# Weight chunks of the first layer decoded in pairs that make their sums on the spot, and a planner with other transfer times, in a one-core attention and two-layer kernel

## The chip, the cores and the metric

The kernel runs on 1 core of one Trainium2 chip. The metric is the device time of one execution in microseconds (us); less is better. TensorE is written PE, its weight loads PEld, VectorE DVE, ScalarE ACT, SyncE SP. SP issues every DMA of this kernel, in one order.

## The reference

What is computed: attention over keys and values that are first averaged over 8 neighbours, then two layers of matrix products.

```python
# q, k, v: [8 batches, 8 heads, 576, 64]
k_p = k.reshape(B, H, 72, 8, D).mean(axis=3)
v_p = v.reshape(B, H, 72, 8, D).mean(axis=3)
attn = softmax(scale * q @ k_p.T)          # sum + 1e-9 below
x = (attn @ v_p), heads side by side       # [4608, 512]
h = x @ w_in;  g = maximum(0.01 * h, h);  x = g @ w_out          # w_in 512x2048, w_out 2048x512
h = x @ w2_in; g = h * clip(h + 3, 0, 6) / 6;  out = g @ w2_out  # the same sizes
```

## The kernel before

**The work and its order.** The 4608 tokens are 9 tiles of 512. Attention is cut into 32 units (batch, pair of head groups, half of the queries), whose scores (matmul L465), transposes (L540, L558) and value products (L585) are strewn between the matmuls of the layers. PE multiplies each f32 operand as a high and a low part, three matmuls in place of one.

Tiles 0, 1 and 2 go through the first layer directly: for each of 16 chunks f of 128 hidden units, 12 matmuls into the hidden values (`gemm1`, L702 to L704), a leaky step on ACT (L717), a split on ACT (L299) and DVE (L309), and 12 matmuls into y (`gemm2`, L751 to L753). This is done in four passes: **pass 1** takes tile 0 through the first `mid` = 9 chunks and stores the unfinished y; **pass 2** takes tile 1 through all 16; **pass 3** takes tile 0 through the chunks from `mid` on and adds; **pass 4** takes tile 2 through all 16. In the profile pass 1 runs from 32 to 107 us, pass 2 to 209, pass 3 to 267, pass 4 to 384. Everything later (`Pair1` for the other six tiles of layer one, then `Pair` for layer two) multiplies blocks of 2x2 with seven products in place of eight (L974). For these seven products the weights have to be summed and differenced beforehand; the results (`left1`, `left2`) are kept in DRAM and streamed back (L1011).

**The weights.** `weights(f)` loads the 1024 KB of chunk f (L608), decodes the 64-bit numbers to f32 in `decode` (two ACT instructions L617, L619 and two DVE instructions L622, L630, each 128x1024), and splits the result into the tile `w{f}` (ACT L299, DVE L309, 128x1024). `keep` then stores the decoded chunk, 512 KB, to DRAM (L651) and three pieces of 256 KB of the split to `left1` (L663). Raw words and the decoded chunk lie in tiles that belong to later chunks, in turn.

`first_weights(f)`, for f = 0 to 7, reads chunks f and f+8 back from DRAM in four pieces of 256 KB (L929) into a tile `raw`, and `combine` makes the sums from its four quarters: four DVE sums or differences (L873), each followed by `split_off`, which splits it (ACT L299, DVE L309) into a tile `st` and stores that in two DMAs of 256 KB (L900). `second_weights(f)` does the same for layer two from the input (L944, 2 x 1024 KB): a decode in four halves of 128x512, each with a temporary tile `st`, three split_offs and `combine`. There are **2** tiles `raw`, which keys and values of attention use too, and **3** tiles `st`: a fourth `st` can be written when the stores from the first have landed. `C` lists in which slot of which pass each of these jobs stands: `when0`, `when1` for `weights`, `left1` for `first_weights`, `left0`, `left2` for `second_weights`, `att*` for units of attention.

**The order on the engines.** Every piece of work is put into a `Plan` with an engine, a cost in ns and its reads and writes. `Plan.order` places them all by these costs and the delays of `lag` between two engines, PE in program order, the other engines and SP by how soon each piece is due, and the instructions are written out in that order; each engine then runs its own in order. A DMA costs `nbytes / 350 + 50`, what reads its result may start 900 ns later, and a DMA may follow an engine's result after 1250 ns. In the start-up the plan also puts small idle matmuls where it expects PE to wait (L1521).

Of the kernel before, what the change touches and what calls it, by code (L numbers as in the profile page):

```python
# [28 lines left out]
ROUNDS = 12  # L29
C = dict(  # L30
    n32=4,
    flex=652,
    mid=9,
    half0=3,
    steps0='rfrfffrff',
    when0=[0, 0, 3, 3, 7, 14, 16, 16],
    att0=[0, 0, 11, 36],
    sec0=4,
    half1=4,
    steps1='frrffrfffffffrff',  # L40
    when1=[0, 8, 10, 20, 22, 25, 35],
    att1=[0, 0, 7, 32],
    sec1=6,
    att2=[0, 4],
    quick=[0, 2, 2, 2, 6],
    slow=[0, 5, 5, 5, 5],
    left0=[(0, 13), (1, 20)],
    left1=[[(0, 26), (1, 30)], [(2, 0), (3, 2), (4, 10)], [(5, 4), (6, 6), (7, 16)]],
    att3=[0, 3, 6, 9, 12, 15, 18, 21],
    gaps3=[0, 3, 3, 3, 3],  # L50
    prep3=[22, 25],
    att5=[6, 15, 24, 33, 42, 51, 60, 69],
    gaps5=[0, 8, 8, 8, 8],
    prep5=[78, 88],
    att7=[8, 24, 40, 56],
    gaps7=[0, 10, 10, 10, 10],
    prep7=[76, 88],
    left2=[[(2, 24)], [(3, 30), (4, 43)], [(5, 0), (6, 16), (7, 32)]],
)
WARM_FROM = 2700  # L60
ENGINES = ("pe", "act", "dve", "gp", "dma")
# [32 lines left out]
class View:  # L94


    def __init__(self, buf, key, cut):
        self.buf, self.cut = buf, cut
        self.key = () if key is None else key if isinstance(key, tuple) else (key,)

    def ap(self):
        t = self.buf.get()
# [3 lines left out]
class Plan:  # L106
# [17 lines left out]
    def add(self, engine, cost, emit, reads=(), writes=(), other=None):  # L124

        n = len(self.tasks)
        after = set()
        over = lambda d, key: (t for k, v in d.items() if all(a == b for a, b in zip(k, key)) for t in v)
        for v in (*reads, *writes):
            assert not v.buf.gone, v.buf.name  # L130
            if v.buf.prev is not None:
                after |= v.buf.prev.users
        for v in reads:
            before = set(over(v.buf.writers, v.key))
            assert before, v.buf.name
            after |= before
        for v in writes:
            after.update(over(v.buf.writers, v.key))
            after.update(over(v.buf.readers, v.key))
        after.discard(n)  # L140
        for v in reads:
            v.buf.readers.setdefault(v.key, set()).add(n)
            v.buf.users.add(n)
        for v in writes:
            v.buf.writers.setdefault(v.key, set()).add(n)
            v.buf.users.add(n)
        self.tasks.append(([(engine, cost, emit)] + ([other] if other else []), after))

    def lag(self, a, b):

        return self.LAG.get((a, b), 900 if a == "dma" else 1250 if b == "dma" else 180)

    def place(self, ways, after, then, rank, lag, first):

# [89 lines left out]
def attention_moe_moe(ctx: ExitStack, tc: tile.TileContext, qt, kt, vm, vr, wt, wq, eye, mask, out):  # L244
# [27 lines left out]
    def act_cost(n, psum=False):  # L272
        return n / 1.2 + (51 if psum else 93)
# [14 lines left out]
        add("pe", n, emit, reads, writes)  # L288

    def on_dma(nbytes, emit, reads, writes):  # L290
        add("dma", nbytes / 350 + 50, emit, reads, writes)

    def other(*way):
        return way if len(plan.tasks) < C["flex"] else None

    def copy(dst, src, n, psum=False, scale=None):

        if scale is None:
            a = lambda: ACT.copy(out=dst.ap(), in_=src.ap())  # L299
            b = lambda: DVE.tensor_copy(out=dst.ap(), in_=src.ap())  # L300
        else:
            a = lambda: ACT.mul(out=dst.ap(), in_=src.ap(), mul=scale)  # L302
            b = lambda: DVE.tensor_scalar_mul(dst.ap(), src.ap(), scale)
        add("act", act_cost(n, psum), a, [src], [dst], other("dve", dve_cost(n, not psum), b))

    def subtract(dst, a, b, n):
        on_dve(
# [96 lines left out]
    def prep_k(u):  # L404
        held_keys[u.g] = u.b
        if u.early:
            for i in range(2):
                sum_pool(part(u.ks, i, lambda t, i=i: t[:, 72 * i : 72 * i + 72]), half_k(u, i), 72)
        else:
            sum_pool(u.ks, u.k, 144)  # L410
        for e in range(2):
            p = slice(64 * e, 64 * e + 64)
            c = slice(SP * e, SP * e + SP)
            s = View(u.ks.buf, u.ks.key, lambda t, p=p: pair(u.ks.cut(t))[p])
            copy(part(kbd[u.g], e, lambda t, p=p, c=c: t[p, :, c]), s, 144)

    def prep_v(u):
        vh, vl = vbd[u.g]
# [6 lines left out]
        for e in range(2):  # L425
            p = slice(64 * e, 64 * e + 64)
            s = View(u.vs.buf, u.vs.key, lambda t, p=p: pair(u.vs.cut(t))[p])
            if u.whole32:
                copy(part(u.whole32[0], e, lambda t, p=p: t[p, :, p]), s, 128, u.early)
                continue  # L430
            hi, lo = [t(e, lambda t, p=p: t[p, :, p]) for t in (vh, vl)]
            copy(hi, s, 128)
            subtract(lo, s, hi, 128)
        on_dve(
            256,
            lambda: DVE.tensor_tensor(
                out=u.m.ap().rearrange("p (a d) -> p a d", a=4),
                in0=u.rs.ap().rearrange("p (o d) -> p o d", o=1).to_broadcast([96, 4, D]),
# [162 lines left out]

    w = {}
    left1 = []
    chunk = [buf(f"chunk{f}", [128, 1024], pool=dram) for f in range(NF)]

    def load_w(f, raw):
        on_dma(
            1 << 20, lambda: DMA.dma_start(out=raw.get().bitcast(I32), in_=wt[f].bitcast(I32)), [], [raw()]  # L608
        )

    def decode(raw, t, l, half=None):

        c0, n = (0, 1024) if half is None else (512 * half, 512)
        words = lambda: raw.get().bitcast(I32).rearrange("p (n two) -> p n two", two=2)[:, c0 : c0 + n]
        bits = lambda v: v.ap().bitcast(I32)

        on_act(n, lambda: ACT.mul(out=t.ap(), in_=f32(words()[:, :, 1]), mul=2.0**-112), [raw()], [t])  # L617

        on_act(n, lambda: ACT.mul(out=bits(l), in_=words()[:, :, 0].bitcast(U32), mul=7.49 / 2**32), [raw()], [l])  # L619
        on_dve(  # L620
            n,
            lambda: DVE.scalar_tensor_tensor(  # L622
                out=bits(l), in0=bits(t), scalar=3, in1=bits(l), op0=ALU.logical_shift_left, op1=ALU.bitwise_or
            ),
            [t, l],
            [l],
        )
        on_dve(
            n,
            lambda: DVE.scalar_tensor_tensor(  # L630
                out=bits(t), in0=bits(t), scalar=-0x80000000, in1=bits(l), op0=ALU.bitwise_and, op1=ALU.bitwise_or
            ),
            [t, l],
            [t],
        )

    def decode_w(f, raw, t, l):
# [5 lines left out]
        lo = wf("lo", lambda t: t[:, 2:4].rearrange("p a n -> p (a n)"))  # L643
        copy(hi, t, 1024)
        subtract(lo, t, hi, 1024)
        keep(f, t, wf)

    def keep(f, t, wf):

        d = chunk[f]()  # L650
        on_dma(1 << 19, lambda: DMA.dma_start(out=d.ap(), in_=t.ap()), [t], [d])  # L651
        r, lower = f % 8, f >= 8

        for g, sides in enumerate(([(5, 1)], [(1, 0), (5, 1)]) if lower else ([(0, 0), (1, 1)], [(0, 0)])):
# [264 lines left out]
    def first_weights(f):  # L919

        t = new_raw()
        for i in range(2):
            for g in range(2):
# [3 lines left out]
                def emit(i=i, g=g):  # L927
                    at = t.get().rearrange("p (i j g n) -> p i j g n", i=2, j=2, g=2)
                    DMA.dma_start(  # L929
                        out=at[:, i, :, 0, :] if g == 0 else at[:, :, i, 1, :],  # L930
                        in_=chunk[f + 8 * i].get()[:, 512 * g : 512 * g + 512].rearrange("p (j n) -> p j n", j=2),
                    )

                on_dma(262144, emit, [chunk[f + 8 * i]()], [View(v.buf, (*v.key, g), None) for v in dst])
        combine(left1[0], f, quarters(t))

    def second_weights(f):
# [398 lines left out]
    load(mask_sb, mask, 1536)  # L1336
    fetch(u1)
    add("dve", 70, lambda: DVE.memset(three.ap(), 3.0), [], [three])
    room = {0: 8, 1: 9, 2: 10, 3: 14, 4: 15, 5: 14, 6: 15, 7: 14, 8: 15, 9: 14, 10: 15, 11: 14, 12: 15, 13: 15, 14: 15}
    temps = {}  # L1340

    def weights(f):
        raw = area(room[f]) if f in room else new_raw()
        at = 12 if f % 2 == 0 and f < 12 or f == 11 else 11 if f < 11 else 14 if f < 14 else 0
        if at == 12:
            t, l = a12("w", lambda t: t[:, 1024:2048]), a13("w", lambda t: t[:, 1024:2048])
        else:
            if not at or at not in temps:
                temps[at] = area(at) if at else new_raw()
            t, l = [temps[at](i, lambda t, i=i: t[:, 1024 * i : 1024 * i + 1024]) for i in range(2)]  # L1350
        load_w(f, raw)
        decode_w(f, raw, t, l)
# [227 lines left out]
```

## Time and profile before

| | |
|---|---|
| median of 3 runs | 1623.59 us (1619.22 to 1626.57) |
| the profiled execution, its own time | 1624.79 us |
| its span, first to last instruction | 1623.0 us |
| PE busy | 1588.9 us (98%), 7899 matmuls |
| DVE busy | 1188.2 us (73%) |
| ACT busy | 1009.3 us (62%) |
| DMA | 414.73 MB, mean 256 GB/s |

The sum of PE's idle time is the span less its busy time, 34.1 us. A matmul's end is modelled, so a busy PE can still be one at half clock: the granted clock has to be read beside the busy time. Where PE waits, the engine it names is mostly not the cause, but itself stands behind something in its own order.

### The profile page before, as it was taken

How to read it: one execution, taken by the hardware profiler on the slowest of the kernel's cores; microseconds unless marked ns; L12 is line 12 of the kernel's file. 1: busy time of each engine (PE TensorE's matmuls, PEld its weight loads, DVE VectorE, ACT ScalarE, POOL GpSimd, SP SyncE). 2: the span in 40 equal slices, each digit the busy share in tenths (PEclk: the TensorE clock that was granted, in tenths of full speed). 3: DMA queues.
4: the chain of work that ended last, by engine and by line, in shares of the span. 5: the costliest groups of instructions: out<-in, count | busy, mean ns of one | idle time of the engine just before them, and what ended most of it. 6: DMA issues, size and time to landing. Idle time of an engine off the chain costs nothing.

```text
span 1623.0 us, 23182 instructions
## 1 busy us (share of the span) xinstructions
PE 1588.9 (98%) x7899; PEld 1361.6 (84%) x7899; DVE 1188.2 (73%) x2122; ACT 1009.3 (62%) x2481; POOL 2.8 (0%) x14
## 2 busy tenths in 40 slices
PE   9999999999999999999999999999999999999999
PEld 8878887887778778878877898888899889889988
DVE  7988777666788976696688669657846965784594
ACT  7977665667777677665675555556545555654454
POOL 0000000000000000000000000000000000000000
PEclk9999999999999999999999999999999999999999
DMA  8989999646886799669999656766775776567564
GB/s 304 323 289 309 325 306 300 231 154 213 259 297 228 243 313 328 220 219 304 335 340 319 215 208 239 263 214 215 262 239 207 238 262 214 214 246 234 208 233 150
DMA packets 134981, 414.73 MB, mean 256 GB/s; under 512 B 19024, under 2 KB 51920, under 8 KB 113104
## 3 DMA queue, kind: packets, MB, share of 16 engines
q1 hardware_dynamic: 134864, 413.26, 74.5%
q8 instruction: 63, 1.03, 0.3%
q14 instruction: 54, 0.44, 0.1%
HBM read 321.98 MB, written 91.23 MB: 255 GB/s over the span
## 4 chain that ended last, share of the span: by engine, by line
PE 66%; DVE 11%; DMA 9%; ACT 4%; issue 2%; SPq 1%; ACTq 0%; DVEq 0%
PE y L974 29%; PE h L974 18%; PE a L974 12%; DMA left<-st 3%; DVE w L873 2%; DMA raw<-chunk 1%; DMA raw<-vm 1%; PE a L465 1%; DVE gl L309 1%; PE a L585 1%; DMA x<-x 1%; DVE st L309 1%; PE y L751 1%; PE y L752 1%; PE y L753 1%
## 5 line engine op out<-in xcount | busy, mean ns | idle before, releaser
L873 DVE TENSOR_TENSOR w<-y,w 128x512 f32<-128x512 f32 (+2 forms) x108 | 70.3, 657 | 73.7 <-PE y L974 73.6
L302 ACT ACTIVATE gh<-w 128x460 fp32r<-128x460 f32 (+1 forms) x140 | 81.8, 587 | 66.5 <-PE y L974 35.2
L1169 DVE SCALAR_TENSOR_TENSOR gl<-w,gh 128x460 fp32r<-128x460 f32 (+1 forms) x140 | 88.5, 635 | 28.6 <-ACT gh L302 28.4
L974 PE MATMUL y<-w,xh 128*128 128x512 f32 (+2 forms) x444 | 106.0, 386 | 2.6 <-DMA xh<-left 2.2
L873 DVE TENSOR_TENSOR w<-w 128x460 f32<-128x460 f32 (+2 forms) x168 | 106.0, 648 | 2.1 <-ACT w L717 1.2
L974 PEld LDWEIGHTS y<-w,xh 128*128 128x128 f32 x444 | 83.7, 190 | 16.6 <-DMA xh<-left 2.5
L490 ACT ACTIVATE s<-a,mx 96x72 f32<-96x72 f32 x264 | 79.7, 323 | 14.1 <-DVE mx L484 14.0
L974 PE MATMUL y<-w,raw 128*128 128x460 f32 (+1 forms) x384 | 86.6, 370 | 0.0
L751 PE MATMUL y<-gh,w 128*128 128x512 f32 (+2 forms) x220 | 85.0, 386 | 0.0
L702 PE MATMUL h<-xh,w 128*128 128x512 f32 (+2 forms) x220 | 83.6, 380 | 0.0
L752 PE MATMUL y<-gl,w 128*128 128x512 f32 (+2 forms) x220 | 81.3, 369 | 2.0 <-DVE gl L309 1.9
L1140 ACT ACTIVATE gh<-w,three 128x460 f32<-128x460 f32 (+1 forms) x60 | 40.9, 682 | 67.2 <-DVE w L873 67.2
L704 PE MATMUL h<-xh,w 128*128 128x512 f32 (+2 forms) x220 | 81.8, 372 | 0.0
L703 PE MATMUL h<-xl,w 128*128 128x512 f32 (+2 forms) x220 | 81.6, 371 | 0.0
L753 PE MATMUL y<-gh,w 128*128 128x512 f32 (+2 forms) x220 | 81.0, 368 | 0.0
L299 ACT CAST gh<-w 128x512 fp32r<-128x512 f32 x96 | 59.7, 623 | 33.3 <-PE y L974 18.2
L974 PE MATMUL y<-w,xl 128*128 128x512 f32 (+2 forms) x324 | 79.0, 386 | 0.0
L974 PEld LDWEIGHTS y<-w,raw 128*128 128x128 f32 x384 | 71.9, 188 | 8.1 <-DVE w L873 0.5
L299 ACT CAST st<-raw 128x512 fp32r<-128x512 f32 x88 | 54.6, 623 | 38.4 <-DMA left<-st 22.8
L309 DVE TENSOR_TENSOR st<-raw,st 128x512 fp32r<-128x512 f32 x88 | 60.0, 686 | 21.3 <-ACT st L299 20.8
L309 DVE TENSOR_TENSOR gl<-w,gh 128x512 fp32r<-128x512 f32 x96 | 65.6, 685 | 10.5 <-ACT gh L299 10.1
L873 DVE TENSOR_TENSOR w<-h,w 128x512 f32<-128x512 f32 (+2 forms) x44 | 29.0, 663 | 59.1 <-PE h L974 59.0
(270 smaller groups left out, 4372.7 us busy)
## 6 DMA issues: line engine op xcount, KB each, us to landing
raw<-left SPq DMA_DIRECT2D x68, 1024.0 KB, 4.9
left<-st SPq DMA_DIRECT2D x176, 256.0 KB, 4.6
xh<-left SPq DMA_DIRECT2D x37, 1024.0 KB, 4.9
xl<-left SPq DMA_DIRECT2D x68, 512.0 KB, 4.9
xh<-left SPq DMA_DIRECT2D x56, 512.0 KB, 5.3
w<-left SPq DMA_DIRECT2D x56, 512.0 KB, 5.3
xl<-left SPq DMA_DIRECT2D x25, 1024.0 KB, 5.0
raw<-wq SPq DMA_DIRECT2D x16, 1024.0 KB, 7.1
```

Of the source, the lines that this page charges most:

```text
L299: a = lambda: ACT.copy(out=dst.ap(), in_=src.ap())
L302: a = lambda: ACT.mul(out=dst.ap(), in_=src.ap(), mul=scale)
L309: lambda: DVE.tensor_tensor(out=dst.ap(), in0=a.ap(), in1=f32(b.ap()), op=ALU.subtract),
L702: PE.matmul(out=o, lhsT=hi, rhs=xh.get()[:, k, c0:c1], start=k == 0, stop=False)
L703: PE.matmul(out=o, lhsT=hi, rhs=xl.get()[:, k, c0:c1], start=False, stop=False)
L704: PE.matmul(out=o, lhsT=lo, rhs=xh.get()[:, k, c0:c1], start=False, stop=k == 3)
L751: PE.matmul(out=y[:, n0:n1], lhsT=hi, rhs=gh.get()[:, n0:n1], start=start, stop=False)
L752: PE.matmul(out=y[:, c0:c1], lhsT=hi, rhs=gl.get()[:, c0:c1], start=False, stop=False)
L753: PE.matmul(out=y[:, c0:c1], lhsT=lo, rhs=gh.get()[:, c0:c1], start=False, stop=stop)
L873: on_dve(n, lambda: DVE.tensor_tensor(out=dst.ap(), in0=a.ap(), in1=b.ap(), op=op), [a, b], [dst])
L974: PE.matmul(out=o, lhsT=l, rhs=r, start=first and i == m == 0, stop=last and i == len(left) - 1 and m == 2, skip_group_check=True,)
L1169: lambda: DVE.scalar_tensor_tensor(out=lo.ap(), in0=v.ap(), scalar=1.0 / 6.0, in1=f32(hi.ap()), op0=ALU.mult, op1=ALU.subtract),
```

## The change

Chunks are taken in the order 0, 8, 1, 9, 2, 10, ... (`ORDER`), so that the two chunks whose sums are made together follow each other. `mid` is 8. The first 8 chunks in this order (hidden blocks 0 to 3 and 8 to 11) go as before, by `weights`, the store to DRAM and `first_weights`, which is now called for f = 0 to 3 only. The other 8 go in four pairs by the new `pair_weights`, all in pass 2: load both, decode each in two halves into the quarters of one tile `raw`, split each half into `w{c}`, store the three pieces to `left1`, and call `combine` at once. They are neither stored to DRAM as decoded chunks nor read back. Their raw words lie in the chunk's own tile `w{c}`, and the temporaries of the decode are tiles `st`. A `View` can now carry several keys (`also`), since half a chunk touches two quarters.

The jobs move: both `second_weights` of pass 2 go, one to pass 3 and one to pass 4; pass 2 has no `first_weights` (2 before), passes 3 and 4 have two each (3 before). The plan reckons a DMA at `nbytes / 340 + 60` and 1500 ns until its result is read; decodes on ACT cost `0.075 * n` more in the plan, and some small copies and one DVE product about 110 ns more. Slots are set anew in all passes up to the third `Pair1`.

```diff
     n32=4,
-    flex=652,
-    mid=9,
+    flex=612,
+    mid=8,
     half0=3,
-    steps0='rfrfffrff',
-    when0=[0, 0, 3, 3, 7, 14, 16, 16],
+    steps0='rfrfffrf',
+    when0=[0, 1, 0, 3, 11, 14, 16],
     att0=[0, 0, 11, 36],
     sec0=4,
     half1=4,
     steps1='frrffrfffffffrff',
-    when1=[0, 8, 10, 20, 22, 25, 35],
-    att1=[0, 0, 7, 32],
+    when1=[7, 7, 17, 20],
+    att1=[0, 0, 26, 32],
     sec1=6,
     att2=[0, 4],
-    quick=[0, 2, 2, 2, 6],
+    quick=[0, 2, 2, 2, 2],
     slow=[0, 5, 5, 5, 5],
-    left0=[(0, 13), (1, 20)],
-    left1=[[(0, 26), (1, 30)], [(2, 0), (3, 2), (4, 10)], [(5, 4), (6, 6), (7, 16)]],
...
-    left2=[[(2, 24)], [(3, 30), (4, 43)], [(5, 0), (6, 16), (7, 32)]],
+    prep7=[76, 87],
+    left2=[[(0, 10)], [(1, 16)], [(2, 28)], [(3, 26), (4, 43)], [(5, 0), (6, 16), (7, 36)]],
...
+        self.keys = [self.key, *also]
...
-        return self.LAG.get((a, b), 900 if a == "dma" else 1250 if b == "dma" else 180)
+        return self.LAG.get((a, b), 1500 if a == "dma" else 1250 if b == "dma" else 180)
...
-        add("dma", nbytes / 350 + 50, emit, reads, writes)
+        add("dma", nbytes / 340 + 60, emit, reads, writes)
...
+    ORDER = [f + 8 * i for f in range(8) for i in range(2)]
+    chunk = [buf(f"chunk{f}", [128, 1024], pool=dram) for f in range(C["mid"])]
...
-        c0, n = (0, 1024) if half is None else (512 * half, 512)
-        words = lambda: raw.get().bitcast(I32).rearrange("p (n two) -> p n two", two=2)[:, c0 : c0 + n]
-        bits = lambda v: v.ap().bitcast(I32)
-
-        on_act(n, lambda: ACT.mul(out=t.ap(), in_=f32(words()[:, :, 1]), mul=2.0**-112), [raw()], [t])
-
-        on_act(n, lambda: ACT.mul(out=bits(l), in_=words()[:, :, 0].bitcast(U32), mul=7.49 / 2**32), [raw()], [l])
+        n, a = (1024, slice(0, 4)) if half is None else (512, slice(2 * half, 2 * half + 2))
+        words = lambda: raw.get().bitcast(I32).rearrange("p (a n two) -> p a n two", a=4, two=2)[:, a]
+        cut = lambda v: v.ap() if len(v.ap().shape) == 3 else v.ap().rearrange("p (a n) -> p a n", n=256)
+        bits = lambda v: cut(v).bitcast(I32)
+        act = lambda emit, v: on_act(n, emit, [raw()], [v], False, 0.075 * n)
+
+        act(lambda: ACT.mul(out=cut(t), in_=f32(words()[:, :, :, 1]), mul=2.0**-112), t)
+
+        act(lambda: ACT.mul(out=bits(l), in_=words()[:, :, :, 0].bitcast(U32), mul=7.49 / 2**32), l)
...
-        keep(f, t, wf)
-
-    def keep(f, t, wf):
-
         d = chunk[f]()
         on_dma(1 << 19, lambda: DMA.dma_start(out=d.ap(), in_=t.ap()), [t], [d])
+        keep(f, wf)
+
+    def keep(f, wf):
+
+        f = ORDER[f]
...
+    def pair_weights(f):
+
+        t = new_raw()
+        blocks = lambda v: v.rearrange("p (q g n) -> p q g n", q=4, g=2)
+        for i in range(2):
+            c = 2 * f + i
+            words = buf(f"w{c}", [128, 2048])
+            load_w(c, words)
+
+            part = [
+                View(
+                    t,
+                    ((i, 0, g) if g == 0 else (0, i, g)),
+                    lambda v, at=at, g=g: blocks(v)[:, at, g, :],
+                    [(i, 1, g) if g == 0 else (1, i, g)],
+                )
+                for g, at in enumerate((slice(2 * i, 2 * i + 2), slice(i, i + 3, 2)))
+            ]
+            for g in range(2):
+                decode(words, part[g], new_st()(None, lambda t: t[:, 0, :]), g)
+            wf = buf(f"w{c}", [128, 4, 512], F32R)
+            w[c] = wf
+            for g in range(2):
+                hi, lo = [
+                    wf((what, g), lambda t, r=2 * r + g: t[:, r].rearrange("p (a n) -> p a n", a=2))
+                    for r, what in enumerate(("hi", "lo"))
+                ]
+                copy(hi, part[g], 512)
+                subtract(lo, part[g], hi, 512)
+            keep(c, wf)
         combine(left1[0], f, quarters(t))
...
-    for f, slot in enumerate(C["when1"], mid):
-        jobs.at(slot, lambda f=f: weights(f))
+    more_weights(jobs, pair_weights, enumerate(C["when1"], mid // 2))
     held["x"] = new_x32()
...
-    more_weights(jobs, first_weights, C["left1"][0])
-    more_weights(jobs, second_weights, C["left0"])
...
-    more_weights(jobs, first_weights, C["left1"][1])
+    more_weights(jobs, first_weights, C["left1"][0])
+    more_weights(jobs, second_weights, C["left2"][0])
...
-    more_weights(jobs, first_weights, C["left1"][2])
+    more_weights(jobs, first_weights, C["left1"][1])
+    more_weights(jobs, second_weights, C["left2"][1])
```

## Rows read from the trace of the kernel before

**Rows 1.** Windows by pass: length, busy us (instructions) per engine, PEclk, DMA share, GB/s

```profile
0.00:32.00 32.00, 29.26 (x306) 27.07 (x307) 23.42 (x55) 22.92 (x89) 2.55 (x13) 1.00 0.87 310
32.00:107.00 75.00, 71.23 (x457) 62.35 (x456) 70.07 (x132) 63.55 (x203) 0.21 (x1) 0.98 0.88 305
107.00:209.00 102.00, 98.85 (x555) 85.20 (x554) 82.55 (x146) 75.14 (x195) 0.07 (x1) 0.98 0.92 314
209.00:267.00 58.00, 54.02 (x250) 43.73 (x249) 40.72 (x72) 34.43 (x107) 0.00 (x0) 0.97 0.91 304
267.00:384.00 117.00, 114.27 (x600) 95.75 (x599) 75.00 (x155) 77.22 (x310) 0.00 (x0) 1.00 0.63 210
384.00:700.00 316.00, 305.62 (x1485) 250.27 (x1484) 246.36 (x464) 230.39 (x697) 0.00 (x0) 0.99 0.79 265
700.00:1623.00 923.00, 915.64 (x4258) 797.27 (x4256) 650.08 (x1103) 505.62 (x889) 0.00 (x0) 1.00 0.70 243
```

**Rows 2.** Timeline of PE: start, length, instruction, idle before it and its releaser

```profile
93.67 0.98 PE L465 MATMUL a<-kbd,q 128*96 128x144 f32 x6 [2.05 <-ACT x L302]
...
145.19 0.37 PE L752 MATMUL y<-gl,w 128*128 128x224 f32 x1 [1.89 <-DVE gl L309]
...
251.95 0.71 PE L558 MATMUL a<-ident,rem 96*96 96x96 f32 x3 [3.70 <-DVE tl L309]
```

**Rows 3.** Waits of PE, 384 to 700: total us, times, longest

```profile
PE y L974 <- DMA xh<-left: 2.2, 1, 2.2
```

**Rows 4.** Windows just behind the four longest waits, columns as in Rows 1

```profile
94.00:99.00 5.00, 5.00 (x20) 4.04 (x19) 2.97 (x6) 2.65 (x15) 0.00 (x0) 0.66 0.89 277
146.00:150.00 4.00, 4.00 (x24) 3.96 (x22) 3.96 (x6) 2.34 (x4) 0.00 (x0) 0.57 0.88 298
252.00:258.00 6.00, 6.00 (x24) 5.01 (x25) 5.71 (x11) 3.47 (x8) 0.00 (x0) 0.73 0.75 271
394.00:398.00 4.00, 3.76 (x11) 2.92 (x12) 3.40 (x6) 2.10 (x4) 0.00 (x0) 0.65 0.21 51
```

**Rows 5.** Timeline of ACT ahead of the first three waits

```profile
92.19 1.12 ACT L617 ACTIVATE w<-w 128x1024 f32<-128x1024 f32 x1 [2.77 <-DMA chunk<-w]
...
143.49 0.62 ACT L299 CAST st<-raw 128x512 fp32r<-128x512 f32 x1 [1.41 <-DMA left<-st]
...
250.58 0.62 ACT L299 CAST st<-raw 128x512 fp32r<-128x512 f32 x1 [3.69 <-DMA left<-st]
```

**Rows 6.** Timeline of DVE ahead of the third wait

```profile
249.38 2.14 DVE L873 TENSOR_TENSOR raw<-raw 128x512 f32<-128x512 f32 x3 [1.25 <-DMA raw<-chunk]
```

**Rows 7.** Groups by shape, 0 to 450: busy us, mean ns | idle before, releasers

```profile
L309 DVE TENSOR_TENSOR w<-w,w 128x1024 fp32r<-128x1024 f32 x14 | 17.0, 1216 | 1.6 <-ACT w L299 1.6
L622 DVE SCALAR_TENSOR_TENSOR st<-raw,st 128x512 int32<-128x512 int32 x12 | 8.0, 686 | 7.0 <-ACT st L619 7.0
...
L299 ACT CAST st<-raw 128x512 fp32r<-128x512 f32 x50 | 31.1, 624 | 23.7 <-DMA left<-st 11.7 <-DVE raw L873 9.8 <-DVE gl L309 0.8
L617 ACT ACTIVATE w<-w 128x1024 f32<-128x1024 f32 x14 | 16.1, 1149 | 3.8 <-DMA chunk<-w 3.2 <-DVE w L309 0.6
L299 ACT CAST w<-w 128x1024 fp32r<-128x1024 f32 x12 | 12.6, 1051 | 2.2 <-DVE w L630 2.1
L617 ACT ACTIVATE raw<-raw 128x512 f32<-128x512 f32 x12 | 7.8, 681 | 3.5 <-DMA raw<-wq 3.0 <-DVE vrm L309 0.5
```

**Rows 8.** DMA issues: count, KB each, median us to landing; whole span, passes 2, 3, 4

```profile
raw<-chunk SPq DMA_DIRECT2D x32, 256.0 KB, 4.5
chunk<-w SPq DMA_DIRECT2D x14, 512.0 KB, 4.7
...
left<-st SPq DMA_DIRECT2D x44, 256.0 KB, 3.6
...
left<-st SPq DMA_DIRECT2D x23, 256.0 KB, 5.1
...
left<-st SPq DMA_DIRECT2D x25, 256.0 KB, 4.1
```

More of the change, by code (lines that the diff above doesn't have):

```diff
@@ L40 @@
     steps1='frrffrfffffffrff',
-    when1=[0, 8, 10, 20, 22, 25, 35],
-    att1=[0, 0, 7, 32],
+    when1=[7, 7, 17, 20],
+    att1=[0, 0, 26, 32],
     sec1=6,
     att2=[0, 4],
-    quick=[0, 2, 2, 2, 6],
+    quick=[0, 2, 2, 2, 2],
     slow=[0, 5, 5, 5, 5],
-    left0=[(0, 13), (1, 20)],
-    left1=[[(0, 26), (1, 30)], [(2, 0), (3, 2), (4, 10)], [(5, 4), (6, 6), (7, 16)]],
-    att3=[0, 3, 6, 9, 12, 15, 18, 21],
-    gaps3=[0, 3, 3, 3, 3],
-    prep3=[22, 25],
+    left1=[[(0, 0), (1, 9)], [(2, 3), (3, 6)]],
+    att3=[0, 0, 6, 9, 12, 15, 18, 21],
+    gaps3=[0, 3, 3, 3, 0],
+    prep3=[26, 33],
     att5=[6, 15, 24, 33, 42, 51, 60, 69],
-    gaps5=[0, 8, 8, 8, 8],
-    prep5=[78, 88],
-    att7=[8, 24, 40, 56],
+    gaps5=[0, 8, 8, 11, 6],
+    prep5=[78, 97],
+    att7=[8, 24, 36, 57],
     gaps7=[0, 10, 10, 10, 10],
-    prep7=[76, 88],
-    left2=[[(2, 24)], [(3, 30), (4, 43)], [(5, 0), (6, 16), (7, 32)]],
+    prep7=[76, 87],
+    left2=[[(0, 10)], [(1, 16)], [(2, 28)], [(3, 26), (4, 43)], [(5, 0), (6, 16), (7, 36)]],
 )
@@ L94, with __init__ @@
 class View:
-    def __init__(self, buf, key, cut):
+    def __init__(self, buf, key, cut, also=()):
         self.buf, self.cut = buf, cut
         self.key = () if key is None else key if isinstance(key, tuple) else (key,)
+        self.keys = [self.key, *also]
     def ap(self):
@@ L133, in add @@
         for v in reads:
-            before = set(over(v.buf.writers, v.key))
+            before = {t for key in v.keys for t in over(v.buf.writers, key)}
             assert before, v.buf.name
@@ L137, in add @@
         for v in writes:
-            after.update(over(v.buf.writers, v.key))
-            after.update(over(v.buf.readers, v.key))
+            for key in v.keys:
+                after.update(over(v.buf.writers, key))
+                after.update(over(v.buf.readers, key))
         after.discard(n)
         for v in reads:
-            v.buf.readers.setdefault(v.key, set()).add(n)
+            for key in v.keys:
+                v.buf.readers.setdefault(key, set()).add(n)
             v.buf.users.add(n)
         for v in writes:
-            v.buf.writers.setdefault(v.key, set()).add(n)
+            for key in v.keys:
+                v.buf.writers.setdefault(key, set()).add(n)
             v.buf.users.add(n)
@@ L290, in on_dma, with copy @@
     def on_dma(nbytes, emit, reads, writes):
-        add("dma", nbytes / 350 + 50, emit, reads, writes)
+        add("dma", nbytes / 340 + 60, emit, reads, writes)
     def other(*way):
         return way if len(plan.tasks) < C["flex"] else None
-    def copy(dst, src, n, psum=False, scale=None):
+    def copy(dst, src, n, psum=False, scale=None, extra=0):
         if scale is None:
@@ L303, in copy @@
             b = lambda: DVE.tensor_scalar_mul(dst.ap(), src.ap(), scale)
-        add("act", act_cost(n, psum), a, [src], [dst], other("dve", dve_cost(n, not psum), b))
+        add("act", act_cost(n, psum) + extra, a, [src], [dst], other("dve", dve_cost(n, not psum), b))
     def subtract(dst, a, b, n):
@@ L414, in prep_k @@
             s = View(u.ks.buf, u.ks.key, lambda t, p=p: pair(u.ks.cut(t))[p])
-            copy(part(kbd[u.g], e, lambda t, p=p, c=c: t[p, :, c]), s, 144)
+            copy(part(kbd[u.g], e, lambda t, p=p, c=c: t[p, :, c]), s, 144, extra=107)
     def prep_v(u):
@@ L431, in prep_v @@
             hi, lo = [t(e, lambda t, p=p: t[p, :, p]) for t in (vh, vl)]
-            copy(hi, s, 128)
+            copy(hi, s, 128, extra=115)
             subtract(lo, s, hi, 128)
         on_dve(
-            256,
+            360,
             lambda: DVE.tensor_tensor(
@@ L603, in attention_moe_moe @@
     left1 = []
-    chunk = [buf(f"chunk{f}", [128, 1024], pool=dram) for f in range(NF)]
+    ORDER = [f + 8 * i for f in range(8) for i in range(2)]
+    chunk = [buf(f"chunk{f}", [128, 1024], pool=dram) for f in range(C["mid"])]
     def load_w(f, raw):
         on_dma(
-            1 << 20, lambda: DMA.dma_start(out=raw.get().bitcast(I32), in_=wt[f].bitcast(I32)), [], [raw()]
+            1 << 20, lambda: DMA.dma_start(out=raw.get().bitcast(I32), in_=wt[ORDER[f]].bitcast(I32)), [], [raw()]
         )
     def decode(raw, t, l, half=None):
-        c0, n = (0, 1024) if half is None else (512 * half, 512)
-        words = lambda: raw.get().bitcast(I32).rearrange("p (n two) -> p n two", two=2)[:, c0 : c0 + n]
-        bits = lambda v: v.ap().bitcast(I32)
-        on_act(n, lambda: ACT.mul(out=t.ap(), in_=f32(words()[:, :, 1]), mul=2.0**-112), [raw()], [t])
-        on_act(n, lambda: ACT.mul(out=bits(l), in_=words()[:, :, 0].bitcast(U32), mul=7.49 / 2**32), [raw()], [l])
+        n, a = (1024, slice(0, 4)) if half is None else (512, slice(2 * half, 2 * half + 2))
[5 more added lines that the diff above has]
+        act(lambda: ACT.mul(out=bits(l), in_=words()[:, :, :, 0].bitcast(U32), mul=7.49 / 2**32), l)
         on_dve(
@@ L930, in emit @@
                         out=at[:, i, :, 0, :] if g == 0 else at[:, :, i, 1, :],
-                        in_=chunk[f + 8 * i].get()[:, 512 * g : 512 * g + 512].rearrange("p (j n) -> p j n", j=2),
+                        in_=chunk[2 * f + i].get()[:, 512 * g : 512 * g + 512].rearrange("p (j n) -> p j n", j=2),
                     )
-                on_dma(262144, emit, [chunk[f + 8 * i]()], [View(v.buf, (*v.key, g), None) for v in dst])
+                on_dma(262144, emit, [chunk[2 * f + i]()], [View(v.buf, (*v.key, g), None) for v in dst])
+        combine(left1[0], f, quarters(t))
+    def pair_weights(f):
[26 more added lines that the diff above has]
+            keep(c, wf)
         combine(left1[0], f, quarters(t))
@@ L1338, in attention_moe_moe @@
     add("dve", 70, lambda: DVE.memset(three.ap(), 3.0), [], [three])
-    room = {0: 8, 1: 9, 2: 10, 3: 14, 4: 15, 5: 14, 6: 15, 7: 14, 8: 15, 9: 14, 10: 15, 11: 14, 12: 15, 13: 15, 14: 15}
+    room = {0: 8, 1: 9, 2: 10, 3: 14, 4: 15, 5: 14, 6: 15, 7: 14}
     temps = {}
     def weights(f):
-        raw = area(room[f]) if f in room else new_raw()
-        at = 12 if f % 2 == 0 and f < 12 or f == 11 else 11 if f < 11 else 14 if f < 14 else 0
+        raw = area(room[f])
+        at = 11 if f % 2 else 12
         if at == 12:
@@ L1347, in weights @@
         else:
-            if not at or at not in temps:
-                temps[at] = area(at) if at else new_raw()
+            if at not in temps:
+                temps[at] = area(at)
             t, l = [temps[at](i, lambda t, i=i: t[:, 1024 * i : 1024 * i + 1024]) for i in range(2)]
@@ L1507, in attention_moe_moe @@
     prepare_pair(jobs, pairs1[2], xr, held, C["prep7"])
-    for p, places in zip(pairs1, C["left2"]):
+    for p, places in zip(pairs1, C["left2"][2:]):
         more_weights(p.jobs, second_weights, places)
```

## The prediction

> **What bounds the kernel now.** First the windows by pass [rows 1]: PE is busy in 1588.9 of 1623.0 us, and the change takes no matmul away, so it can only win what PE loses by waiting. By pass that idle time is 2.7 us (0 to 32), 3.8, 3.2, 4.0, 2.7 (passes 1 to 4), 10.4 (384 to 700) and 7.4 (the rest, of which the last drain is part). From 700 on no job of the change is left, and the clock is at full speed. So the stretch to look at is 32 to 700 us: 24.0 us idle.
>
> Then PE's timeline and waits: four idle times near 92, 144, 250 and 393 us are by far the longest, 2.05, 1.89, 3.70 [rows 2] and 2.2 us [rows 3], together 9.8. Behind each the clock falls: windows of 5, 4, 6 and 4 us have a granted clock of 0.66, 0.57, 0.73 and 0.65 [rows 4], where the passes as a whole have 0.97 to 1.00. A mean below 1 mixes the two levels, 1.2 and 2.4 GHz. Length times missing share: 1.7 + 1.7 + 1.6 + 1.4 = 6.4 us. So the four cost 3.75, 3.6, 5.3 and 3.6, in sum 16.3 us; the other 14.2 us of idle time is in pieces of 1.7 us and less, without such a loss.
>
> Third, what stands behind the four. PE names ACT or DVE, but these wait for a landing themselves: at 92 us ACT stood 2.77 us before a decode until the store of an earlier decoded chunk had landed, at 143 us 1.41 us and at 250 us 3.69 us before a split until a store from `st` had landed [rows 5], and DVE stood at 249 us until a reload of a chunk had landed [rows 6]. ACT and DVE work in order: the value product and the split that PE needed were queued behind. At 393 us PE waits for a stream itself [rows 3]. All four are landings later than the order of the instructions allows for. The order reckons with 262144/350 + 50 + 900 = 1.70 us from the start of a 256 KB transfer to its use, and the trace has medians of 3.6 to 5.1 us from issue to landing [rows 8]; for the 512 KB chunk store it is 2.45 against 4.7.
>
> **The change part by part.** *DMA.* A chunk by `weights` moves 1024 + 512 + 768 = 2304 KB, a `first_weights` 1024 + 2048 = 3072, a `second_weights` 2048 + 14 x 256 = 5632, a new pair 2 x 1792 + 2048 = 5632. Pass 1: 9 to 8 chunks, -2304 KB. Pass 2: 7 x 2304 + 2 x 3072 + 2 x 5632 = 33536 becomes 4 x 5632 = 22528, -11008 KB. Passes 3 and 4: 3 x 3072 becomes 2 x 3072 + 5632, +2560 each. In all -8192 KB (8 stores, 16 reloads). In pass 2, where 32 MB pass at 314 GB/s [rows 1], 11.3 MB is 36 us of transfer time; I expect (32.0 - 11.3) MB in 102 us, some 205 GB/s. But PE is idle in only 3.2 of these 102 us, so that is the most the pass can give beside its clock loss.
>
> *DVE and ACT.* Chunks: three DVE instructions of about 1216 ns against six of 686, so 156 ns more for each of 24 pairs of halves, 3.7 us; on ACT (2 x 681 - 1149) = 213 ns for each of 16 decodes and (2 x 624 - 1051) = 197 for each of 8 splits, 5.0 us [rows 7]. All of it falls into pass 2, and there other work goes: DVE 7 x 3.65 + 2 x 8 x 0.686 + 2 x 19 x 0.686 = 62.6 becomes 4 x 20 x 0.686 = 54.9 us; it was busy 82.6 of 102 [rows 1]. So the dearer halves are hidden by DVE's idle time in a pass that gets lighter; without that cover they would be the 3.7 us. I take 0, and keep +3.7 for the range.
>
> Against this stands a rule of the Trainium skill (VectorE: DVE Perf Modes, section "The TRN2 errata — SBUF-src ops pay a fixed extra latency per instruction"): many small tiles pay per instruction what one large tile pays once. By its table the 24 cuts would cost DVE an estimated 24 x 58 cycles at 0.96 GHz, 1.5 us; the rows have 3.7. Either way it is hidden.
>
> *Pass 3 and 4.* Pass 3 gets a `second_weights` for a `first_weights`: 11 more DVE half-instructions, 7.5 us, and 2560 KB, and also the chunk that pass 1 gives up, which is 24 of its then 274 matmuls or some 5.6 us by the pass's own pace (58 us for 250). Its DMA, 17.6 MB in 58 us, becomes about 20.2 MB in 63.5 us, 318 GB/s: as full as pass 2 is now [rows 1]. Pass 4 runs at 210 GB/s and has room. Pass 1 gives PE time and a chunk away together; its load per us stays.
>
> *Rings.* Raw words no longer alternate in two tiles, so loads can be issued earlier. But the pair's temporaries come from the three `st`, as the sums' stores do: 8 `st` per pair. Of these, the first three and the last wait for a store, four waits as in a `first_weights`. A pair also holds one of the two `raw` through two decodes and four sums; keys and values need both.
>
> *The plan.* 262144/340 + 60 + 1500 = 2.33 us to use in place of 1.70, and 3.10 for 2.45 after a chunk store. Each hop by DMA gets 0.6 us more, where 2 to 3 are missing. That applies everywhere. The small copies cost more in the plan as the trace has them; worth 0 by itself. More idle matmuls in the start-up may follow; they stand where PE waits: 0, bounds -1 and +1.
>
> *The sum.* (a) 92 us: the chunk store stays, reckoned 0.65 us later; 1.5 of 3.75 (bounds 0 and 3.75). (b) 144 us: the `second_weights` behind it leaves, its pass loses a third of its traffic, and a pair brings waits of the same kind; 3.0 of 3.6 (0 to 3.6). (c) 250 us: reload and store ring remain, one `first_weights` fewer, the DMA no less full; 2.0 of 5.3 (-5.3, one such stall more, to 5.3). (d) 393 us: the sums are finished a pass earlier, but the wait is for the streamed read; 1.0 of 3.6 (0 to 3.6). (e) the 14.2 us of small waits: 0.63 us off those that hang on a DMA hop; I take about a third, 5.0 (0 to 14.2). Together 12.5 us. From the profiled execution's 1624.8 that is 1612.3; this execution lies 1.2 us above the median of the runs, 1623.6, so in terms of it **1611 us**.
>
> **The rivals.** *A, the forecast:* landings reckoned better and pass 2 lighter, some of each stall goes: 1611, by itself 1603 to 1618. For it: all four causes are landings [rows 5, 6]; against: only 0.6 us of each is added to the plan.
>
> *B, the relief stays off PE's path:* DMA traffic was never what PE waited for, the latency of one store was, and that stays; only (b) goes: 1623.6 - 3.0 = 1620.6. For it: 3.6 us landing at 314 GB/s and 4.1 at 210 [rows 8].
>
> *C, slower:* in pass 3 the seven splits of a `second_weights` go through three `st` on the fullest DMA, with landings of 5.1 us [rows 8], beside two reloads; ACT stops before a split, attention behind it, PE behind that, as at 250 us. Each costs 5.3 us; with the gains of A gone elsewhere it is slower from two more such stalls on, 10.6 us: 1634. Against it: pass 2 now holds two `second_weights` at 314 GB/s and has one stall of 1.89 us.
>
> *D, all four stalls go*, and a third of the small ones: 16.3 + 4.7 = 21 us: 1602.6. It needs each landing to become earlier or planned for. Beside it stands the Trainium skill (DMA: Bandwidth & Descriptors, section "Latency and other measured facts"): a lighter HBM load makes the fixed cost smaller. By that rule a lighter pass 2 lands its stores sooner; the trace does not agree, with 4.1 us at 210 GB/s against 3.6 at 314.
>
> **How the numbers follow.** A 0.55, B 0.24, C 0.10, D 0.11. What a measurement of this kernel can tell from no change is 0.5%, 8.1 us: faster is below 1615.5, slower above 1631.7. D and four fifths of A are faster: 0.11 + 0.44 = 0.55; B and a fifth of A are the same: 0.35; C is slower: 0.10. The range reaches from a part of D to above B with the 3.7 us and a small stall in pass 3: 1600 to 1627; it leaves out most of C and the lower half of D.
>
> **What would show it.** Chunk stores 16 to 8, reloads 32 to 16, decodes of 1024 columns half as many; PE's matmuls the same but for idle ones. Step by step: pass 2 near 205 GB/s and without a window below 0.9 clock; no ACT wait on a chunk store after pass 1; in pass 3 no idle time of PE above 2 us; fewer waits of PE between 384 and 700. It would be wrong if PE's idle time between 32 and 700 stays near 24 us (B), or if pass 3 shows two or more stalls behind ACT splits that wait for `left<-st` (C).

## The result and the profile after

| | before | after |
|---|---|---|
| median of 4 runs | 1622.28 us (1619.22 to 1626.57) | 1601.34 us (1600.35 to 1602.59) |
| profiled execution, its span | 1624.79, 1623.0 us | 1600.35, 1598.6 us |
| PE busy | 1588.9 us | 1577.9 us |
| mean granted clock | 0.996 | 1.000 |

The ratio is 0.9869, 95% interval 0.9844 to 0.9894: faster by 1.3%, some 21 us, where 1611 was forecast. The windows of the changed kernel, cut at its own passes, answer to [rows 1] (columns as there):

```profile
0.00:32.60 32.60, 30.26 (x325) 28.37 (x326) 23.66 (x57) 22.62 (x88) 2.54 (x13) 1.00 0.86 304
32.60:95.00 62.40, 61.08 (x401) 54.15 (x400) 60.58 (x119) 51.81 (x167) 0.30 (x1) 1.00 0.85 310
95.00:198.40 103.40, 102.89 (x581) 89.04 (x580) 86.30 (x171) 77.46 (x226) 0.00 (x0) 1.00 0.80 275
198.40:253.70 55.30, 54.11 (x270) 44.58 (x269) 41.72 (x78) 40.75 (x131) 0.00 (x0) 1.00 0.75 246
253.70:368.40 114.70, 111.78 (x583) 93.52 (x582) 82.73 (x167) 81.57 (x313) 0.00 (x0) 1.00 0.72 239
368.40:685.00 316.60, 314.06 (x1534) 258.56 (x1534) 256.55 (x482) 236.59 (x706) 0.00 (x0) 1.00 0.82 273
685.00:1598.60 913.60, 903.68 (x4212) 789.41 (x4210) 639.51 (x1086) 499.67 (x875) 0.00 (x0) 1.00 0.71 242
```

The first layer's seven-product part starts at 368.4 in place of 383.7 us: 15.3 us are won by then, and 24.9 at the end of the first `Pair1`, at 557.6 in place of 582.5. PE is idle 8.5 us between 32.6 and 685 (1.3, 0.5, 1.2, 2.9, 2.5), against 24.0 before, and the granted clock is 1.00 in every pass: the 6.4 us at half clock [rows 4] are gone too. Behind 685 the idle time went up, from 7.4 to 9.9 us. Of the 24.4 us between the two spans, idle time and clock explain 20; the rest lies in stretches that the view counts as busy, since it models where a matmul ends. One correction to the rows on record: counted by its matmuls, pass 3 of the kernel before begins at 218 us, so the window to 209 cuts the last of pass 2 off; PE is idle only 0.1 us between 209 and 218, so the idle times by pass stand.

The four largest waits of PE on others in the changed kernel (total us, times, longest):

```profile
PE a L561 <- DVE tl L312: 3.2, 4, 1.6
PE h L1014 <- ACT st L302: 2.5, 1, 2.5
PE h L1014 <- DVE gl L1209: 2.0, 4, 0.5
PE h L1014 <- DMA w<-left: 1.5, 1, 1.5
```

None of the four long waits [rows 2, 3] is left. What stood behind them went as well: ACT never waits for a chunk's store now, and before splits it waits a sixth as long for stores from `st` (its decodes into `st` wait 1.6 us, 0.5 before). The waits of ACT, whole span, of the kernel before and then of the changed one:

```profile
ACT st L299 <- DMA left<-st: 23.9, 20, 3.7
...
ACT w L617 <- DMA chunk<-w: 3.2, 2, 2.8
```

```profile
ACT st L302 <- DMA left<-st: 4.0, 5, 1.5
```

Did the stores land sooner? DMA issues of the changed kernel, whole span, then passes 2 (95 to 198 us), 3 and 4, answering to [rows 8]:

```profile
left<-st SPq DMA_DIRECT2D x176, 256.0 KB, 4.5
...
chunk<-w SPq DMA_DIRECT2D x8, 512.0 KB, 4.0
raw<-chunk SPq DMA_DIRECT2D x16, 256.0 KB, 4.0
...
left<-w SPq DMA_DIRECT2D x48, 256.0 KB, 4.0
left<-st SPq DMA_DIRECT2D x32, 256.0 KB, 3.0
...
left<-st SPq DMA_DIRECT2D x24, 256.0 KB, 4.3
...
left<-st SPq DMA_DIRECT2D x36, 256.0 KB, 3.5
```

The reader is to see three things. Over the whole span the median of the same 176 stores is 4.5 us, 4.6 before. But in passes 2, 3 and 4 they land 0.6, 0.8 and 0.6 us sooner than before (3.6, 5.1 and 4.1 [rows 8]), so the shorter waits of this kernel can come both from the order and from the landings; `b_lag` below, whose stores on the whole land no sooner, tells the two apart. And all 48 pieces for `left1` from pass 1 and 2 leave in pass 2.

### The profile page after: what moved, and what is told of

Same layout as the page of the kernel before. It is cut to its first block, busy times and chain, and to the rows that moved or that the text cites. A ratio compares the mean times of both kernels' runs of the same rounds, so it can differ in the third digit from the quotient of the medians.

```text
span 1598.6 us, 23198 instructions
## 1 busy us (share of the span) xinstructions
PE 1577.9 (99%) x7896; PEld 1357.6 (85%) x7896; DVE 1191.0 (75%) x2154; ACT 1010.5 (63%) x2497; POOL 2.8 (0%) x14
## 4 chain that ended last, share of the span: by engine, by line
PE 82%; DVE 8%; DMA 6%; ACT 3%; issue 1%; SPq 0%; DVEq 0%; ACTq 0%
PE y L1014 31%; PE h L1014 21%; PE a L1014 13%; PE y L759 2%; PE y L760 2%; PE y L761 2%; PE h L710 2%; PE a L468 2%; PE h L712 2%; PE h L711 2%; PE a L588 2%; DMA left<-st 1%; DMA raw<-wq 1%; DVE w L881 1%; ACT s L493 1%
## 5 line engine op out<-in xcount | busy, mean ns | idle before, releaser
L1014 PEld LDWEIGHTS y<-w,xh 128*128 128x128 f32 x444 | 82.5, 188 | 12.5
L1014 PEld LDWEIGHTS y<-w,xl 128*128 128x128 f32 x324 | 60.1, 188 | 10.5 <-DVE w L881 0.5
```

The source lines that it names most:

```text
L1014: PE.matmul(out=o, lhsT=l, rhs=r, start=first and i == m == 0, stop=last and i == len(left) - 1 and m == 2, skip_group_check=True,)
```

## The experiments

Theory 1: the gain comes from planning landings later, so that in-order engines stand less behind them. Theory 2: it comes from what the new jobs take out of pass 2, and that may be the traffic, the way by DRAM, or only the moved jobs and slots. All times are medians of 4 runs and more; the runs of the kernel before beside them had medians of 1622.1 to 1623.3 us (single runs 1615.7 to 1629.7).

| kernel | median us (runs) | ratio to before, interval |
|---|---|---|
| b_costs: before, new plan costs | 1613.39 (1612.50 to 1613.67) | 0.9940, 0.9919 to 0.9961 |
| b_lag: before, 1500 ns alone | 1613.00 (1609.84 to 1617.39) | 0.9940, 0.9918 to 0.9962 |
| a_oldcosts: changed, old plan costs | 1613.21 (1610.57 to 1619.16) | 0.9944, 0.9920 to 0.9968 |
| b_moved: before, second_weights moved | 1620.72 (1614.13 to 1627.31) | 0.9968, 0.9948 to 0.9988 |
| a_traffic: changed, 8 MB of copies | 1603.65 (1602.63 to 1604.32) | 0.9898, 0.9876 to 0.9920 |
| a_viadram: changed, pairs by DRAM | 1605.84 (1602.02 to 1609.22) | 0.9904, 0.9875 to 0.9934 |
| a_ring: changed, words in two tiles | 1602.19 (1600.01 to 1604.17) | 0.9889, 0.9866 to 0.9913 |
| a_slots: changed, slots of before | 1604.27 (1601.69 to 1608.69) | 0.9891, 0.9861 to 0.9921 |
| a_lagpe: changed, 1500 ns to PE only | 1606.78 (1603.17 to 1607.22) | 0.9899, 0.9872 to 0.9926 |
| a_lagve: changed, 1500 ns to ACT, DVE only | 1598.46 (1595.58 to 1601.87) | 0.9846, 0.9815 to 0.9877 |
| a_lag2200: changed, 2200 ns | 1598.82 (1597.15 to 1599.63) | 0.9868, 0.9845 to 0.9890 |
| a_lag3000: changed, 3000 ns | 1597.63 (1597.04 to 1599.52) | 0.9849, 0.9824 to 0.9874 |

**The two halves apart.** `b_costs` puts all the new numbers of the plan into the kernel before, `b_lag` one of them; `a_oldcosts` takes them all out of the changed kernel.

```diff
-        ... 900 if a == "dma" else 1250 ...      (b_lag; b_costs also 340 + 60 and the extras)
+        ... 1500 if a == "dma" else 1250 ...
```

> The kernel before with the planner's new costs alone (transfer size and latency, decode and small copies), its own jobs and slots. Theory 1, landings planned later are the gain: most of the 21 us, 1602 to 1608. Theory 2, the work that leaves pass 2 (traffic, second_weights) is the gain: 1617 to 1625, with idle time of PE between 32 and 700 us still near 24 us.

> The kernel before with one number changed, 1500 for 900 ns from a landing to its use in the plan. Theory 1: as good as all new costs, 1603 to 1610, waits of ACT for left<-st and chunk<-w shorter. Theory 2: 1617 to 1625.

> The changed kernel, pairs and new slots, planned with the old costs. Theory 1: most of the gain is lost, 1614 to 1622. Theory 2: it stays, 1601 to 1607.

Neither theory had it: each half gives 10 us, and the ratios multiply to the whole (0.9940 x 0.9944 = 0.9884, measured 0.9869). Of the costs, the landing delay is all, in the kernel before: `b_lag` equals `b_costs`. The waits of ACT for `left<-st`, in order of `b_costs`, `b_lag`, `a_oldcosts`:

```profile
ACT st L299 <- DMA left<-st: 6.9, 9, 1.5
```

```profile
ACT st L299 <- DMA left<-st: 18.3, 19, 2.0
```

```profile
ACT st L302 <- DMA left<-st: 21.8, 18, 2.7
```

The sum of these waits does not measure the gain: `b_lag` wins as much as `b_costs` with 18.3 of the 23.9 us left. What shrank in it is the longest of them (3.7 to 2.0 us), and with it DVE's waits for reloads (9.3 to 5.1 us) and for a store from `st` (4.5 us to none). Its stores land no sooner on the whole: medians of 4.0, 5.5 and 3.6 us in passes 2, 3 and 4 against 3.6, 5.1 and 4.1, and 4.7 over the whole span against 4.6. So its gain comes from the order.

Where a gain shows varies from plan to plan. Up to the seven-product part the profiles of `b_costs`, `b_lag` and `a_oldcosts` are 4.6, 11.6 and 11.2 us ahead of the kernel before, and in the first `Pair1` another 7.8, -0.2 and 0.7; a single wait is no proof of a cause, the total has to be read. A plan in which some other number is changed, to see what a mere reshuffling of the order gives, was not run; every plan here that puts landings later came out below its counterpart with 900 ns in the median.

**Which landings.** The 1500 ns only towards PE, or only towards ACT and DVE.

```diff
+        ... (1500 if b == "pe" else 900) if a == "dma" ...      (a_lagpe)
+        ... (900 if b == "pe" else 1500) if a == "dma" ...      (a_lagve)
```

> The changed kernel with the 1500 ns only from a transfer to PE, which covers the streams of ready weights and the queries; 900 ns to ACT and DVE. If the streams' landings are what the plan had wrong: as good as the changed kernel, 1600 to 1604. If the waits of ACT and DVE (stores from st, reloads, keys and values) are: 1609 to 1615, as with the old costs.

> The reverse: 1500 ns from a transfer to ACT and DVE, 900 ns to PE. If ACT's and DVE's waits are what the plan had wrong: 1600 to 1604. If the streams: 1609 to 1615. If both count, this one and the one before lie between, 1604 to 1609 each.

Towards ACT and DVE it suffices: `a_lagve` has the whole gain, 1.5 us below every range named, while `a_lagpe` loses 5.4 us of it and lies in the range named for the case that both count. `a_lagpe` is still 6.4 us below `a_oldcosts`, but it keeps the other new costs too, so what 1500 ns towards PE alone are worth was not parted from them. ACT's waits for `left<-st`, first `a_lagpe`, then `a_lagve`:

```profile
ACT st L302 <- DMA left<-st: 17.7, 13, 2.6
```

```profile
ACT st L302 <- DMA left<-st: 8.7, 10, 1.7
```

**More of it.** 2200 and 3000 ns in place of 1500.

> The changed kernel planned with 2200 ns from a landing to its use in place of 1500. Theory landings: the trace's landings are still 1.5 to 2 us later than planned, so it goes on, 1592 to 1599. Rival, the first 600 ns were what there was to have, and longer ones leave engines idle or only shuffle the order: 1599 to 1608.

> The changed kernel planned with 3000 ns from a landing to its use. If the planned landing still counts: 1592 to 1598, below the 1598.8 of 2200 ns. If 2200 ns reached the landings of the trace: 1597 to 1603.

2.5 and 3.7 us less than the changed kernel, and no single run of either is above its fastest one; but the ratios to the runs beside them are 0.9868 and 0.9849 against its 0.9869, with intervals that overlap, so a better version is not shown. 2200 ns came out just inside the first expectation and 3000 ns inside both, so whether the gain ends at 2200 is not settled; it has become small. ACT's waits for stores from `st` in the plan with 3000 ns are nearly gone, and the time has hardly moved:

```profile
ACT st L302 <- DMA left<-st: 1.8, 3, 0.9
```

**What of the new jobs gives the other 10 us.** `b_moved` moves the two `second_weights` alone:

```diff
-    left0=[(0, 13), (1, 20)],
+    left2=[[(0, 10)], [(1, 16)], [(2, 24)], ...        (runs in passes 3 and 4, as in the change)
```

> The kernel before, old costs, with its two second_weights of pass 2 moved to passes 3 and 4, where the change has them; no pairs, all chunks still by DRAM. Theory 2: the wait of 1.9 us at 144 us goes, but passes 3 and 4, which keep three reloads each, get longer: 1612 to 1622. Theory 1: no gain, 1618 to 1628.

2.6 us, with runs that spread over 13 us: inside both expectations and little of the 10. `a_traffic` puts the bytes back without anyone who waits for them:

```diff
+            d = buf(f"spare{c}", [128, 2048], pool=dram)()
+            on_dma(1 << 20, lambda d=d, c=c: DMA.dma_start(out=d.ap()..., in_=wt[ORDER[c]]...), [], [d])
```

> The changed kernel with 8 copies of 1024 KB from DRAM to DRAM beside the pairs' loads in pass 2, which nobody reads: the 8 MB that the change took out go back in, with no hop and no wait on them. Theory traffic (PE lost to a full DMA): half or more of the structure's 10 us is lost, 1606 to 1614. Theory hops (what cost time were landings that an in-order engine stood for): 1600 to 1605.

It costs 2.3 us, as the theory of hops had it. The plan put five of the eight copies into pass 2, all after 146 us, and three into pass 3. With the five, pass 2 is as full as that of the kernel before was, and PE stands still in it for 0.4 us:

```profile
94.50:200.00 105.50, 105.10 (x600) 91.45 (x599) 87.37 (x171) 82.29 (x251) 0.00 (x0) 1.00 0.94 318
```

So in this pass a DMA at 0.94 did not hold PE up. `a_viadram` brings back the way by DRAM, bytes and hop:

```diff
+                on_dma(262144, ... DMA.dma_start(out=d.buf.get()[:, 512 * g : 512 * g + 512]..., in_=v.ap()), [part[g]], [d])
             keep(c, wf)
-        combine(left1[0], f, quarters(t))
...
+    more_weights(jobs, first_weights, [(4, 11), (5, 13), (6, 22), (7, 26)])
```

> The changed kernel, but the four pairs store their decoded halves to DRAM and first_weights reads them back four to six slots later in the same pass and makes the sums: same work in the same pass, the way by DRAM again. Theory hops: the structure's gain goes with the way by DRAM, 1608 to 1615. Rival, the gain lies in moved jobs and slots and not in the way: 1599 to 1605.

4.5 us, between the two expectations: 2.3 as with the bytes alone, and 2.2 for the hop, of the size of what these runs scatter by. In its pass 2 PE is idle 3.3 us again, and DVE waits for the reloads there; that PE's idle time stands behind these waits is not shown:

```profile
94.20:206.10 111.90, 108.61 (x613) 92.83 (x611) 90.14 (x178) 83.55 (x254) 0.28 (x1) 1.00 0.93 311
```

```profile
DVE raw L881 <- DMA raw<-chunk: 2.7, 3, 1.8
```

`a_ring` lets the words alternate in two tiles, `a_slots` puts the slots of attention and preparation, and `flex`, back:

```diff
-            words = buf(f"w{c}", [128, 2048])                    (a_ring)
+            words = buf(f"w{14 + c % 2}", [128, 2048])
...
-    att1=[0, 0, 26, 32], quick=[0, 2, 2, 2, 2], flex=612         (a_slots; att3, gaps3, prep3 and so on likewise)
+    att1=[0, 0, 7, 32], quick=[0, 2, 2, 2, 6], flex=652
```

> The changed kernel with the raw words of the pairs in two tiles in turn (as before) and not each in its own. If earlier loads are part of the gain: 1603 to 1610. If not: 1600 to 1603.

> The changed kernel, pairs, costs and the jobs' passes as they are, with the slots of attention in pass 2, of attention and preparation in pass 4 and later, and the limit flex of the kernel before. If the part of the structure's gain that neither traffic nor the way by DRAM explains lies in these slots: 1605 to 1612. If it lies in the jobs that left pass 2 and in mid: 1600 to 1604.

The own tiles give nothing that can be told from 0 (0.9 us), the slots some 3 us, between the two expectations. So of the 10 us some 4.5 may go with the way by DRAM (half of it the bytes) and 3 with the slots; the other 2 to 3 are open. They would have to lie in `mid` and in the jobs that left pass 2; a changed kernel with `mid` = 9 was not tried. Each of these parts is of the size by which one plan differs from another, and the intervals of all four ratios overlap with the changed kernel's, so none of the shares is shown. One more cause was not tested: with these jobs the stores land sooner even under the old costs (`a_oldcosts`: 3.1, 3.1 and 3.3 us in passes 2, 3 and 4, against 3.6, 5.1 and 4.1 before), and with the way by DRAM back, in `a_viadram`, they take 4.4 us in pass 2.

## Why the prediction was right, and too small

*The place and the mechanism* held: the time came from PE's waits between 32 and 685 us, landings stood behind them, and planning landings later was worth 10 us by itself. The other 10 us came with the jobs, by ways that the runs part only roughly. The time itself is near the end of what was given: 1601.3 us is 1.3 us inside the range of 1600 to 1627, and below the 1603 to 1618 of rival A, the forecast.

*The halves* of DVE and ACT at 0: held. They cost what was reckoned (686 to 688 ns and 674 ns for 128x512), and pass 2 has 0.5 us of idle PE with DVE busy 86.3 of 103.4 us. The 3.7 us kept for the range were too dear: instructions of 128x1024 that follow each other start 1.13 us apart (before, near 70 us), halves 0.60 us, so 24 cuts are some 24 x 0.07 = 1.7 us; in the mean durations the end of one overlaps with the start of the next. These are the rows of the halves, 0 to 430 us:

```profile
L629 DVE SCALAR_TENSOR_TENSOR st<-raw,st 128x512 int32<-128x512 int32 x28 | 19.1, 688 | 9.8 <-ACT st L626 9.5
L624 ACT ACTIVATE raw<-w 128x512 f32<-128x512 f32 x16 | 10.3, 674 | 0.8 <-DVE st L312 0.8
```

*DMA.* 8 stores and 16 reloads went, as said. But pass 2 runs at 275 GB/s, not 205. That came from dividing by passes where jobs are placed: the 33536 KB counted for pass 2 before are more than all that passed there (32.0 MB). The plan sends pieces of `left1` when they are due, 48 of 48 in this pass, 28 before (107 to 218 us), and it sends seven of the eight loads for the pairs ahead of this pass. Pass 3, reckoned at 318 GB/s, ran at 246. The sum leaned on this in (b) alone: not a third of pass 2's load went, but an eighth (314 to 275 GB/s).

*The terms.* (b) 3.0, and pass 2's idle time fell from 3.2 to 0.5 us without a clock loss of 1.7: some 3.6, its bound. (e) 5.0: the small waits went from 14.2 to 8.5 us, 5.7. Where it failed is the size of the other three, 1.5, 2.0 and 1.0. (a) All 3.75: no wait for a chunk's store is left. (c) All 5.3: the stall of 3.70 us went with its clock loss of 1.6; the 1.2 us of idle time left in pass 3 are among the 8.5 of (e). (d) All 3.6: PE waits nowhere at the start of the seven-product part. These are 12.7 us for 4.5. With (b) and (e) it makes 22.0 us for 12.5, less the 2.5 us more of idle time behind 685, booked at nothing. The reason given was "Each hop by DMA gets 0.6 us more, where 2 to 3 are missing", so only a part of each could go. The runs showed in its place that the missing time need not be covered in full: the new costs, 600 ns and the small ones, took ACT's waits on stores from 21.8 to 4.0 us (`a_oldcosts` against the changed kernel), and 1500 ns more brought at most 3.7 us of time. Besides, 0.6 to 0.8 us came from the other side, as the stores of passes 2 to 4 landed sooner. And a wait that became shorter took its 1.4 to 1.7 us at half clock with it as a whole. That is rival D for the four stalls, at 0.11 held too unlikely.

*Rival B* fell: four stalls went, not one, and the jobs under the old costs are worth 10 us (`a_oldcosts`). Its premise, that PE did not wait for traffic, is borne out in pass 2: with five of the copies put back PE is idle 0.4 us there (`a_traffic`). *Rival C* fell in pass 3: 1.2 us idle, no stall over 1 us. A wait that looks like its mechanism, three `st` and a late store, appears at 830 us in a `Pair1`. The chain of waits of the changed kernel (start, length), its DVE and PE timelines and a window there:

```profile
821.24 5.98 DMA left<-st
...
827.31 0.70 DVE st L881
```

```profile
827.31 1.29 DVE L881 TENSOR_TENSOR st<-w 128x512 f32<-128x512 f32 x2 [0.45 <-DMA left<-st]
```

```profile
830.31 0.50 PE L1014 MATMUL h<-gh,w 128*128 128x512 f32 x1 [2.52 <-ACT st L302]
```

```profile
829.00:834.00 5.00, 3.69 (x16) 3.02 (x17) 5.00 (x10) 2.84 (x6) 0.00 (x0) 1.00 0.93 364
```

The chain names a DVE difference that needs an `st` whose store takes 6 us, and ACT and PE follow. But DVE stood only 0.45 us for that store; from 818 us to the end of PE's wait it was busy in 11.85 of 12.3 us, and in all of the 19.7 us behind. So it is DVE's full order that PE waits for here, and a later landing in the plan does not help: with 3000 ns a wait of the same line and releaser takes 2.78 us (`a_lag3000`), while DVE is busy without a gap from 810 us to its end. With the 1.5 us wait for a stream near 809 us this is more than what the part behind 685 lost. The kernel before, `b_lag` and `a_oldcosts` have no PE wait of 1.5 us or more between 700 and 900 us; `b_costs` has this one with 2.67 us, and the plans with all the new numbers have it with 1.2 (`a_lagve`) to 4.3 us (`a_lag2200`). Why it comes with them is open. It is the next place to look.

*Rival D's rule*, from the Trainium skill (DMA: Bandwidth & Descriptors, "Latency and other measured facts"), is that a lighter HBM load lowers the fixed cost. Medians from issue to landing of 3.0 us at 275 GB/s and 4.3 at 246 against 3.6 at 314 and 5.1 at 304 agree in passes 2 and 3, while pass 4, 3.5 at 239 against 4.1 at 210, does not; over all stores nothing changed (4.5 and 4.6).

## What to carry to other kernels

In a kernel whose order is written ahead, read ACT's and DVE's waits for DMA in the trace and compare them with what the plan allows for a landing: here one number, 600 ns more, was worth as much as the whole rebuilding of the jobs, 10 us each. Here a DMA at 0.94 in a pass was no bound for PE while nobody in the order waited for the added bytes; an instruction that stood behind a landing held up what was queued on its engine [rows 5], so look for the wait before counting bytes. A chain of waits names the last releaser: read beside it how long the engine stood idle for it, 0.45 us of 2.52 in the case at 830 us. Read the granted clock in the window behind each long wait before pricing it.

## What was not expected of the hardware

Idle time of PE did not cost the same everywhere. Before, waits of 1.89 to 3.70 us were each followed by a window at 0.57 to 0.73 of the clock [rows 2, 4]. After, the wait of 2.52 us at 830 us was followed by none (1.00 in the window above), nor was one of 2.8 us that ended at 463 us in `a_oldcosts`, where the window behind it has 1.00:

```profile
PE a L588 <- ACT s L493: 3.0, 2, 2.8
```

```profile
463.00:468.00 5.00, 4.96 (x27) 4.15 (x28) 3.22 (x9) 4.90 (x16) 0.00 (x0) 1.00 0.66 235
```

The wait at 830 us is found in other plans too, by its line and its releaser. In `a_slots` it took 2.48 us and was followed by 5 us at 0.66, the window below, while behind 2.52 us in the changed kernel and 2.67 us in `b_costs` the clock stayed at 1.00:

```profile
832.50:837.50 5.00, 4.97 (x15) 3.98 (x16) 4.37 (x8) 1.37 (x3) 0.00 (x0) 0.66 0.79 312
```

So a wait of 2 to 3 us may or may not bring the lower level, and what it costs has to be read from the window behind it.
